# Transposing gated keys with a 112 × 112 identity in place of a 128 × 128 one, in an HGRN2 attention feeding a bilinear FFN

## The chip, the cores and the metric

The kernel runs on one NeuronCore of one Trainium2 chip. The metric is the device time of one execution in microseconds (us). Before the change it is 597.28 us, the median of three runs (597.1 to 597.85).

## What is computed

The first part is a linear attention with a gate per channel, for 4 batches × 8 heads, 768 tokens, head width 48. Its output, put back into rows of 384 channels, goes through a bilinear feed-forward block (384 → 1536 → 384). All of it is float32, with the FFN weights arriving as doubles.

```python
f = 1.0 / (1.0 + np.exp(-f_logit))
for t in range(S):
    state = f[:, :, t, :, None] * state + np.einsum('bhd,bhe->bhde', k[:, :, t], v[:, :, t])
    y[:, :, t] = np.einsum('bhd,bhde->bhe', q[:, :, t], state)
x = y.transpose(0, 2, 1, 3).reshape(B * S, H * D)
out = (x @ w_a) * (x @ w_b) @ w_out
```

## The kernel before

**Units and their places.** `by_quotients` cuts the attention into 16 units u = 0 to 15: four heads times one block of 384 tokens each. In SBUF a unit's q, k and f are tiles of 128 partitions × 2 × 384. Two heads lie above each other, the one in partitions 0 to 47 and the other in 64 to 111 (R = 64, D = 48); the rows 48 to 63 and 112 to 127 hold padding. v lies with its tokens on the partitions. The names carry the set of buffers that a unit uses, u modulo 3: `k_in` of unit 9 is that of set 0, of unit 10 set 1, of unit 11 set 2.

**The front of a unit** (`front_parts`, lines 302 to 347) makes sigmoids on ScalarE (L312, L315), an affine step on GpSimd (L318), running products and sums as scans on VectorE (L322, L335), and multiplies k and q by them on VectorE (L339). After that the attention of a chunk of 128 tokens is plain matrix products.

**The core of a unit.** `scores` (L392) multiplies k with q in 24 small matrix products and `mask` (L405, VectorE) copies the causal part into `at`. `turn` (L416) transposes the unit's decayed keys, so that tokens come to lie on partitions: 6 TensorE transposes a unit, each with a 128 × 128 block of k as the stationary operand and the identity as the moving one, into one pair of PSUM banks. `turned` (L423 for units 0 and 1, L425 for the others) copies the pair on ScalarE into the SBUF tile `kT`, [128 tokens, 2, 3 chunks, 128]. `gains` (L440) multiplies a 48-column slice of `kT` with v; it reads the columns 0 to 47 and 64 to 111 of a chunk and no others. `carried` or `carry` (L467, L469) sums the gains into running states on VectorE. `within` (L489) and `across` (L515) make the outputs, and `out_of_bank` (L534) with DMAs brings them into `xT`.

**The FFN.** Blocks 0 and 1 of 384 tokens use plain products (`up`, L598, and `product`, L618 and L620). From block 2 on, `up_triples` (L714 to 791) does the product of a 3 × 3 by a 3 × 2 block matrix with 15 multiplications in place of 18. For each of four columns j it makes 15 named products v1, v6 (of the column before), u1, r2, v2, u2, t1, v3, u3, r3, v4, u4, t2, v5, u5, in that order. One named product is one "beat": two matmuls of 192 columns. They go into four PSUM banks (in turn called v, u, r, t), are copied out by ScalarE (`copy`, shown as L1307, where the planner emits it) or added by VectorE (`add` and others, L712), and the next product that uses the bank has to wait for that. `down` (L795, matmuls at L822) multiplies by w_out, two blocks of 128 tokens at a time.

**What sets the order.** Up to unit 3 the order is written out by hand (lines 1002 to 1120). From there a small planner (lines 1138 to 1310) walks along a main list of FFN steps and fills in the attention's steps from lines of their own. It keeps a clock of its own for TensorE (`now`) and for each other engine, adds each step's stated cost to it, and emits a step of a side line when it fits. In `core_parts` (line 901) each step has its cost in nanoseconds: `scores` 1000, `turn` 850, `turned` 700, `gains` 1000. These numbers are no instructions; they decide only where steps stand in the queues. Each engine then runs its own queue in that order, and waits at semaphores.

Of the kernel before, what the change touches and what calls it, by code (L numbers as in the profile page):

```python
# [12 lines left out]
FP32 = mybir.dt.float32  # L13
# [7 lines left out]
C = 128  # L21
FINE = (0, 1, 2, 4, 8, 16)
BLK = 384
# [3 lines left out]
R = 64  # L27
# [115 lines left out]
def by_quotients(ctx, tc, q, k, f_logit, v, moe_w_a, moe_w_b, moe_w_out, out, ident, weights, bad, ps_f):  # L143
    nc = tc.nc
    B, H, D, S = q.shape
# [5 lines left out]
    NC = BLK // C  # L151
# [9 lines left out]
    sb1 = ctx.enter_context(tc.tile_pool(name="sb1", bufs=1))  # L161
# [39 lines left out]
    def unit(u):  # L201
        b, r = divmod(u, NH * NQ)
        return (b, *divmod(r, NQ))
# [89 lines left out]
    PE, DVE, ACT, POOL, SP = range(5)  # L293
    live = {}
# [4 lines left out]
    def halves(x):  # L299
        return x.rearrange("p n s -> p (n s)")  # L300
# [75 lines left out]
    def away(u):  # L376

        return ps_y if u == 2 else ps_x

    def pair_of(x):  # L380

        return [x[:, i] for i in range(2)]
# [25 lines left out]
    def turn(u):  # L408

        kf = halves(sets[u % NSET]["k"])  # L410
        live.setdefault(u, {})["kT"] = sb1.tile([128, 2, NC, 128], FP32, tag="kT", name="kT")
        ps = live[u]["turned"] = [ps_f[idle.pop(0)] for _ in range(2)] if u in FIRST else pair_of(away(u))
        for n in range(2):
            for c in range(NC):
                o = n * BLK + c * C
                nc.tensor.transpose(ps[n][:, c * C:c * C + C], kf[:, o:o + C], ident)  # L416

    def turned(u):

        kT, ps = live[u]["kT"], live[u]["turned"]  # L420
        if u in FIRST:
            for n in range(2):
                nc.scalar.copy(kT[:, n].rearrange("s c x -> s (c x)"), ps[n][:, 0:BLK])  # L423
        else:
            nc.scalar.copy(kT.rearrange("s n c x -> s n (c x)"), away(u)[:, :, 0:BLK])  # L425

    def gains(u, chunks=range(NC)):

# [112 lines left out]
    def stores_of(u):  # L541

        b, half, qd = unit(u)
        blk = b * NH + half

        def begin():
            if qd == 0:
                xT[blk] = sb2.tile([128, NKT, BLK], FP32, tag="xT", name="xT")
            live.pop(u - NQ, None)

        def store(n, h, kt, p, row, w):
            y = live[u]["y_sb"].rearrange("r (n c) p m -> r n (c p m)", n=2)
            queue = nc.sync if u != NQ - 1 else nc.gpsimd if n else nc.scalar
            queue.dma_start(out=xT[blk][p:p + w, kt], in_=y[row:row + w, n])

        yield begin
        for n in range(2):
            for h in range(2):
                ch, row, left = (4 * qd + 2 * n + h) * D, R * h, D
                while left:  # L560
                    kt, p = divmod(ch, 128)
                    w = min(left, 128 - p)
                    yield partial(store, n, h, kt, p, row, w)
                    ch, row, left = ch + w, row + w, left - w
# [336 lines left out]
    def core_parts(s):  # L901


        u = s - 1
        if u < 2 * NQ:
            yield PE, 1000, 0, scores, s
        elif s < NU:
            yield PE, 1600, 0, within_and_scores, u
        else:
            yield PE, 1000, 20 * BEAT, within, u  # L910
        if s < NU:
            yield DVE, 880, 0, mask, s
            yield PE, 850, 0, turn, s
            yield ACT, 700, 0, turned, s
        if u < 2 * NQ:
            yield PE, 1000, 0, gains, s
        elif s < NU:
            yield PE, 1550, 0, gains_and_across, u
        else:
            yield PE, 1000, 0, across, u  # L920
        if s < NU:
            for j in range(NJ - 1 if unit(s)[1] == NH - 1 else NJ):
                yield DVE, 180, 0, carry, s, j
            if unit(s)[1] < NH - 1:
                yield DVE, 320, 0, hand_on, s
        if u >= 2 * NQ:
            for part in range(3):
                yield ACT, 490, 0, out_of_bank, u, part
            begin, *stores = stores_of(u)
            yield SP, 0, 0, begin  # L930
            for do in stores:
                yield SP, ISSUE, 5000, do
# [41 lines left out]
    with tc.manual_schedule():  # L974
# [43 lines left out]
        begin(1)  # L1018
        keep_up(2)
        turn(0)  # L1020
        turned(0)
        scores(0)
        begin(2)
        gains(0)
        keep_up(4)
        for _ in range(3):
            next(fronts[1])
        turn(1)
        turned(1)
        mask(0)  # L1030
        scores(1)
# [154 lines left out]
        for s in range(2 * NQ, NU + 1):  # L1186
            if s < NU:
                loaded = ()
                if s - NSET in stores:
                    at = stores[s - NSET]  # L1190
                    loaded = (loads.extend([(SP, ISSUE, 6000, do) for do in loads_of(s)], needs=(at,)),)
                ready = fore.extend(
                    [(e, load, 0, *do) for part in front_parts(s) for e, load, *do in part], needs=loaded
                )
            for step in core_parts(s):
                blk, second = divmod(s - 1, NQ)
                core.extend(
                    (step,),
                    needs=(ready,) if step[3] in (scores, within_and_scores) else (),
                    past=behind[blk - 2] if step[3] in (across, gains_and_across) and not second else 0,  # L1200
                )
            if s > 2 * NQ:
                stores[s - 1] = core, len(core.steps)
            if s > 2 * NQ and s % NQ == 0:
                blk = s // NQ - 1
                one_by_one = combine_x(blk)
                marks["x", blk] = for_x.extend(
                    [(e, load, 0, next, one_by_one) for e, load in X_STEPS],
                    needs=(stores[s - 1],),
                    past=behind[blk - 1] if blk > 2 else behind["down"],  # L1210
                )
# [448 lines left out]
```

## Time and profile before

| | |
|---|---|
| median of three runs | 597.28 us |
| the profiled execution, as a run | 596.37 us |
| span of the profiled execution | 594.6 us |
| TensorE matmuls busy | 572.6 us (96%) |
| VectorE busy | 412.2 us (69%) |
| ScalarE busy | 268.7 us (45%) |
| mean granted TensorE clock | 0.997 |

The profile is of one execution. The run's time is 1.8 us longer than its span, which begins with the first instruction and ends with the last. A matmul in full float32 has two records in the profile (L598 has 288 for 144 calls); a transpose has one (L416 has 96 for 16 units × 6). The pieces of the chain of waits count a weight load and a matmul each, so that "x4" of L598 there is two passes; in the timeline of one engine "x4" of L720 is one beat. In units of work "PE" is the matmul and "PEld" the weight load that runs beside it.

### The profile page before, as it was taken

To read this page: it belongs to the slowest core of one execution; us is meant where nothing else is said; L and a number is where in the kernel's file an instruction comes from. 1 tells how busy PE (TensorE), PEld (TensorE's weight loads), DVE (VectorE), ACT (ScalarE), POOL (GpSimd) and SP (SyncE) were. 2 spreads that over 40 slices of the span, in tenths; PEclk is the share of its full clock that TensorE was granted. 3 is DMA by queue.
4 is the path that set the end of the run, shared out by engine and by line. 5 is a ranking of instruction groups with operands and counts; after the bars stand their busy time and mean duration, and the time that the engine had idled before them with its cause. 6 is when DMAs were issued, how large, how long until landed. Compare 5 with 4: busy or idle time off the path is not lost.

```text
span 594.6 us, 13952 instructions
## 1 busy us (share of the span) xinstructions
PE 572.6 (96%) x5802; PEld 512.9 (86%) x5802; DVE 412.2 (69%) x786; ACT 268.7 (45%) x507; POOL 77.7 (13%) x71
## 2 busy tenths in 40 slices
PE   2899999999999999999999999999999999999997
PEld 1655655557999999999999999999999999999996
DVE  6899545599978678958894678847785165836751
ACT  6589959753132464245521444326431345135300
POOL 6254425355000000000000000000000000000000
PEclk9899999999999999999999999999999999999999
DMA  9696699089542440044004410041001100000001
GB/s 211 183 267 197 213 273 268 0 147 186 116 141 71 115 93 10 15 120 95 2 1 125 108 23 2 2 105 43 3 1 47 48 1 0 2 28 1 0 29 33
DMA packets 33561, 49.43 MB, mean 83 GB/s; under 512 B 3984, under 2 KB 25264, under 8 KB 33488
## 3 DMA queue, kind: packets, MB, share of 16 engines
q1 hardware_dynamic: 30000, 42.19, 25.5%
q0 software_dynamic: 3056, 5.92, 5.9%
q8 instruction: 47, 0.77, 0.5%
q10 hardware_dynamic: 432, 0.34, 0.2%
q14 instruction: 26, 0.21, 0.1%
HBM read 33.23 MB, written 4.72 MB: 64 GB/s over the span
## 4 chain that ended last, share of the span: by engine, by line
PE 85%; DVE 10%; issue 2%; ACT 1%; DMA 1%; SPq 0%; DVEq 0%; ACTq 0%
PE ps_f L720 35%; PE ps_f L822 28%; PE ps_f L598 13%; PE ps_y L489 2%; DVE inv L335 2%; PE ps_y L515 2%; PE ps_x L392 2%; PE ps_x L440 1%; PE ps_x L416 1%; DVE sums L712 1%; DVE groups L712 1%; DVE spare L335 1%; DVE q_in L339 1%; DVE f_in L322 1%; DVE w_ba L73 1%
## 5 line engine op out<-in xcount | busy, mean ns | idle before, releaser
L598 PE MATMUL ps_f<-xT,w_ba 128*128 128x384 f32 x288 | 95.6, 489 | 1.5 <-DMA xT<-y 1.4
L1307 ACT COPY sums<-ps_f 128x384 f32<-128x384 f32 x120 | 57.4, 480 | 75.9 <-PE ps_f L720 68.2
L598 PEld LDWEIGHTS ps_f<-xT,w_ba 128*128 128x128 f32 x288 | 53.8, 190 | 38.2 <-issue 2.2
L1307 ACT COPY groups<-ps_f 128x384 f32<-128x384 f32 x120 | 57.7, 481 | 62.9 <-PE ps_f L720 39.9
L720 PE MATMUL ps_f<-xT,w_ba 128*128 128x192 f32 x384 | 78.4, 327 | 0.0
L720 PEld LDWEIGHTS ps_f<-xT,w_ba 128*128 128x128 f32 x384 | 64.7, 190 | 0.2
L720 PE MATMUL ps_f<-groups,w_ba 128*128 128x192 f32 x288 | 55.5, 327 | 0.0
L720 PE MATMUL ps_f<-x_sums,raw 128*128 128x192 f32 x288 | 54.1, 331 | 1.2 <-DVE groups L712 0.9
L822 PE MATMUL ps_f<-w_out,sums 128*128 128x192 f32 x288 | 52.2, 329 | 0.3 <-DVE groups L620 0.3
L822 PE MATMUL ps_f<-w_out,groups 128*128 128x192 f32 x288 | 51.7, 328 | 0.0
L720 PEld LDWEIGHTS ps_f<-x_sums,raw 128*128 128x128 f32 x288 | 46.9, 190 | 4.3 <-DVE groups L712 1.8
L822 PE MATMUL ps_f<-spare,sums 128*128 128x192 f32 x288 | 49.0, 326 | 0.0
L720 PEld LDWEIGHTS ps_f<-groups,w_ba 128*128 128x128 f32 x288 | 47.8, 190 | 0.5 <-ACT groups L1307 0.3
L822 PEld LDWEIGHTS ps_f<-w_out,sums 128*128 128x128 f32 x288 | 47.1, 190 | 1.3 <-DVE groups L620 0.6
L318 POOL TENSOR_SCALAR inv<-inv 128x768 f32<-128x768 f32 x14 | 13.1, 935 | 266.7 <-ACT inv L315 266.7
L822 PEld LDWEIGHTS ps_f<-w_out,groups 128*128 128x128 f32 x288 | 47.1, 190 | 0.7
L822 PEld LDWEIGHTS ps_f<-spare,sums 128*128 128x128 f32 x288 | 47.1, 190 | 0.1
L60 POOL TENSOR_SCALAR sums<-sums 128x768 f32<-128x768 f32 (+1 forms) x20 | 40.4, 2018 | 43.9 <-ACT sums L58 43.8
L712 DVE TENSOR_TENSOR sums<-sums,groups 128x768 f32<-128x768 f32 x36 | 34.7, 965 | 14.2 <-ACT groups L1307 13.7
L712 DVE TENSOR_TENSOR sums<-ps_f,sums 128x384 f32<-128x384 f32 x60 | 32.8, 553 | 16.5 <-PE ps_f L720 15.0
L720 PE MATMUL ps_f<-x_sums,w_ba 128*128 128x192 f32 x192 | 39.3, 327 | 0.5 <-DVE sums L712 0.5
L720 PE MATMUL ps_f<-xT,raw 128*128 128x192 f32 x192 | 39.4, 328 | 0.0
(142 smaller groups left out, 869.3 us busy)
## 6 DMA issues: line engine op xcount, KB each, us to landing
raw<-w_ba POOLq DMA_DIRECT2D x11, 512.0 KB, 8.6
k_in<-in_k_dram SPq DMA_DIRECT2D x32, 144.0 KB, 4.2
q_in<-in_q_dram SPq DMA_DIRECT2D x32, 144.0 KB, 4.4
v_in<-in_v_dram SPq DMA_DIRECT2D x16, 288.0 KB, 5.0
raw<-in_moe_w_out_dram SPq DMA_DIRECT2D x6, 768.0 KB, 5.9
out_dram<-o SPq DMA_DIRECT2D x22, 192.0 KB, 1.9
f_in<-in_f_logit_dram SPq DMA_DIRECT2D x28, 144.0 KB, 3.0
xT<-y SPq DMA_DIRECT2D x45, 72.0 KB, 2.2
```

The source lines that it names most:

```text
L60: nc.gpsimd.tensor_scalar(h, h, HI_MAX, None, ALU.min)
L73: nc.vector.tensor_tensor(dst[:, rows], hu[:, rows], bit[:, rows], ALU.add)
L318: nc.gpsimd.tensor_scalar(inv, inv, EXP_K, 1.0, ALU.mult, ALU.add)
L335: nc.vector.tensor_tensor_scan(inv[:, w], inv[:, w], none[:, 0:C], first, ALU.mult, ALU.add)
L392: nc.tensor.matmul(ps[h][SUB * p:SUB * p + SUB, o:o + SUB], lhsT=kf[r, tokens(n, c, p)], rhs=qf[r, tokens(n, c, p)], start=True, stop=True,)
L489: nc.tensor.matmul(ps[p][e:e + D, o:o + SUB], lhsT=t["v"][r, n, c, h * D:h * D + D], rhs=at[r, h, o:o + SUB], start=o == 0, stop=True, ski ...
L515: nc.tensor.matmul(ps[p][e:e + D, o:o + SUB], lhsT=st[j][r, n], rhs=qf[r, tokens(n, c, p)], start=False, stop=True, skip_group_check=True,)
L598: nc.tensor.matmul(ps[nm][:, 0:BLK], lhsT=w[:, kt, ft * 128:ft * 128 + 128], rhs=xT[blk][:, kt], start=kt == 0, stop=kt == NKT - 1,)
L712: nc.vector.tensor_tensor(to, x, y, op)
L720: nc.tensor.matmul(ps[:, g], lhsT=sums_of_w[name][:, g, 128 * j:128 * j + 128], rhs=sums_of_x[blk][name], start=start and g == 0, stop=Tru ...
L822: nc.tensor.matmul(to, lhsT=x[:, i // 2, i % 2], rhs=w[:, NI * (i % 2) + i // 2], start=start and i == 0, stop=i == HFT - 1, skip_group_ch ...
L1307: do(*args)
```

## The change

The transposes read 112 rows of k and 112 × 112 of the identity; the chunks of the turned keys follow each other at 112 columns in PSUM and in `kT`, and the copies move 2 × 336 elements a partition in place of 2 × 384. The stated cost of `turn` in the planner goes from 850 to 760.

```diff
-        live.setdefault(u, {})["kT"] = sb1.tile([128, 2, NC, 128], FP32, tag="kT", name="kT")
+        live.setdefault(u, {})["kT"] = sb1.tile([128, 2, NC, R + D], FP32, tag="kT", name="kT")
         ps = live[u]["turned"] = [ps_f[idle.pop(0)] for _ in range(2)] if u in FIRST else pair_of(away(u))
+        used = ident[0:R + D, 0:R + D]
         for n in range(2):
             for c in range(NC):
                 o = n * BLK + c * C
-                nc.tensor.transpose(ps[n][:, c * C:c * C + C], kf[:, o:o + C], ident)
+                nc.tensor.transpose(ps[n][:, c * (R + D):(c + 1) * (R + D)], kf[0:R + D, o:o + C], used)
...
-                nc.scalar.copy(kT[:, n].rearrange("s c x -> s (c x)"), ps[n][:, 0:BLK])
+                nc.scalar.copy(kT[:, n].rearrange("s c x -> s (c x)"), ps[n][:, 0:NC * (R + D)])
         else:
-            nc.scalar.copy(kT.rearrange("s n c x -> s n (c x)"), away(u)[:, :, 0:BLK])
+            nc.scalar.copy(kT.rearrange("s n c x -> s n (c x)"), away(u)[:, :, 0:NC * (R + D)])
...
-            yield PE, 850, 0, turn, s
+            yield PE, 760, 0, turn, s
```

A comparison of the built queues of both kernels shows what moves. With the new sizes and the old 850, no instruction changes place. With 760, the queues differ in two places of TensorE, both in the planner's part: around unit 9's outputs and unit 10's turn (256 to 263 us in the profile before), where a beat of `up_triples` (v1) comes ahead of `within`, `scores` and what follows; and around unit 10's outputs and unit 11's turn (285 to 291 us), where `within`, `scores` and `turn` come one beat earlier. VectorE's and ScalarE's queues change around the same places by a few steps each.

## The prediction

> **What bounds the kernel.** I read the page first, its busy shares and the chain that ended last.
>
> ```profile
> PE 572.6 (96%) x5802; PEld 512.9 (86%) x5802; DVE 412.2 (69%) x786; ACT 268.7 (45%) x507; POOL 77.7 (13%) x71
> PE 85%; DVE 10%; issue 2%; ACT 1%; DMA 1%; SPq 0%; DVEq 0%; ACTq 0%
> ```
>
> TensorE is the bound: 96% busy, 85% of the chain. The rest of the chain is mostly VectorE: the start up to 50.8 us, where TensorE waits anyway, and three short stretches (222 to 228, 287 to 302, 346 to 357 us). So a transpose off TensorE's queue counts from 50.8 us on, unless VectorE gives the pace just then. Next the rows of the transposes and of their copies:
>
> ```profile
> L416 PEld LDWEIGHTS ps_x<-ident,k_in x78: 139/141/146, 54.5 to 427.3; 128*128 128x128 f32 x78
> L416 PE MATMUL ps_x<-ident,k_in x78: 272/273/273, 54.8 to 427.4; 128*128 128x128 f32 x78
> ```
>
> ```profile
> L425 ACT COPY kT<-ps_x x13: 771/798/818, 56.2 to 427.7; 128x768 f32<-128x768 f32 x13
> ```
>
> The 273 ns are one record's length, not what a transpose costs in a stream. That is read in the timeline of TensorE, from start to start:
>
> ```profile
> 289.67 0.82 PE L416 MATMUL ps_x<-ident,k_in 128*128 128x128 f32 x6
> 290.33 2.35 PE L720 MATMUL ps_f<-x_sums,raw 128*128 128x192 f32 x12
> ```
>
> Six transposes take 290.33 - 289.67 = 0.66 us; the chain gives 0.65 to 0.67 for others, so one step is 109 ns. The row below it is three beats of `up_triples`, usually 2.11 us (at 268.41 and 278.16) and here 2.35: 0.24 us of waiting lie in it. The chain of the same stretch:
>
> ```profile
> 286.95 0.75 PE ps_x L392 x47
> ...
> 288.60 0.95 DVE f_in L322
> 289.55 0.91 DVE sums L712 x2
> 290.46 0.87 DVE f_in L322
> ...
> 291.92 1.32 DVE sums L712 x2
> ...
> 293.32 0.48 ACT groups L1307
> 293.80 0.39 ACT sums L1307
> ...
> 300.53 1.03 DVE groups L712 x2
> 301.55 0.04 issue
> 301.60 1.41 PE ps_f L720 x7
> ```
>
> Here VectorE is full, and TensorE stands idle for 0.86 us ahead of 301.60. But the chain enters VectorE from TensorE, by the scores at 286.95: what TensorE saves before this stretch moves all of it.
>
> **What the Trainium skill says.** "TensorE: Matmul & The Clock Gate", section "LDWEIGHTS (loading the stationary operand)": a weight load takes columns / 1.2 ns, whatever the number of rows. The trace agrees for ordinary weights: 122, 134 and 190 ns for 48, 64 and 128 columns, some 0.85 ns a column above a fixed part. For the transposes it gives less, 141 ns for 128 columns. So cutting the rows of k from 128 to 112 saves nothing in the load; only the moving columns count. Its section "Back-to-back issue gap" has N / 2.4 + 2.5 ns for a lone bf16 stream and says that load and matmul set the spacing together. The trace's float32 passes are slower and the trace decides: 162.5 ns for 192 columns (a beat of 4 passes in 0.65 us), 109 for 128, thus (162.5 - 109) / 64 = 0.84 ns a column. Its "Part 4: PE-mode transpose" gives about 275 ns for a transpose in a kernel; the record here has 273.
>
> **The change, part by part.**
>
> *Transposes.* 16 moving columns fewer at 0.84 ns are 13.4 ns for one, if the stream sets the pace. For it: the steps of 128 and 192 columns lie on one line, the load of a transpose (141 ns long, 60 above the fixed part of the ordinary loads, 122 - 48 x 0.85 = 81) is shorter than its stream. Against: the load of the ordinary matmul behind the sixth has to hide behind a stream of 95 ns in place of 109, and 128 columns at 0.85 are 109. So a turn saves 5 x 13.4 = 67 ns up to 6 x 13.4 = 80; I take 75. The turns of units 0, 1 and 2 (at 13, 19 and 38 us) lie where VectorE makes the chain: nothing, and if that cover were gone, 0.08 us each. The 13 turns of units 3 to 15 save 13 x 0.075 = 0.98 us (0.87 to 1.04).
>
> *Copies.* 482 ns for 384 elements and 798 for 768: 0.82 ns an element, so 672 take 719, 79 ns less. ScalarE is 45% busy and other beats lie between turn and gains, so this hides nearly everywhere. It is on the chain once: at 346.2 the copy of unit 13 stands ahead of the sigmoid L315, the sigmoid ahead of the copies that VectorE needs up to 357.27. I count 0.08 us once (0 to 0.2). If the cover were gone in all 14, 1.1 us more would be saved.
>
> *Reading columns.* `gains` reads the same values at a step of 112 columns; same shapes, nothing.
>
> *The planner's 760.* GpSimd's queue stays as it is, SyncE's keeps its order too; no DMA passes another. Around 256 us a beat (v1) comes ahead of unit 9's `within` and unit 10's `scores`. TensorE has no stall from 256 to 286, and its work there is the same; the mask behind waited 1.34 us, and takes the shift. The copy of the keys then comes some 0.5 us ahead of its gains, as before. Nothing.
>
> Around 286 us `within`, `scores` and `turn` of unit 11 come a beat earlier. Placed by hand with the durations of the trace (before the other savings): `within` 285.35, scores end 287.04 in place of 287.69; the mask waits for them and starts at 287.08, not 287.73. Behind it on VectorE stands now the addition of r3, which before filled the wait (0.46 us). One scan that stood ahead of the k product has moved into an idle 0.34 us at 280.5, so k and q are ready some 0.35 us earlier, by 284.9. Then the scans and additions follow as before: the addition of u4 ends at 289.74, where u5 wants its bank at 290.15. On ScalarE the copy of the keys is done by 290.4, so that the copy of v5 (before from 291.22, with v6 waiting for it: the 0.24 us above) is done by 290.8, and v6 is due at 291.45: that wait goes. VectorE's second addition at 292.29 comes at 291.9 to 292.0. From there to the wait ahead of 301.60 the order is the same, so v1 of the next column starts some 0.3 to 0.4 us earlier. I take 0.38 us. Late next is VectorE itself: the stall before v1 is still about 0.7 us. Bounds: all of it, 0.86 + 0.24 = 1.1 us gained, or 0.6 lost if the moved steps meet a bank a beat too late.
>
> *Sum.* 0.98 + 0.08 + 0.38 = 1.44 us. The span goes from 594.6 to 593.1, the run that was profiled from 596.37 to 594.9. The median of the runs shown is 0.91 us above that run; I take the difference off the median: 597.28 - 1.44 = 595.84, and say 595.8.
>
> 0.2% is 1.19 us, about what a measurement of this kernel can tell from no change.
>
> **Rivals.**
>
> *The load sets the pace.* The stationary operand keeps 128 columns, and 128 at 0.85 ns are 109 ns, just the step that is seen. Then 112 moving columns save nothing, and there remain 0.08 + 0.38: 596.8 us. For it: the agreement of the numbers. Against it: the transposes' own load record, 49 ns shorter than an ordinary one. 0.11.
>
> *VectorE takes it back.* What is saved ahead of a VectorE-bound stretch is waited away in it: turns 3 to 13 count for nothing, the two behind 357 us save 0.15, with 0.08 and 0.38: 596.7 us. For it: three stretches where TensorE waits for VectorE. Against: each of them is entered from TensorE, at 222.2 by a copy, at 287.7 by the scores, at 346.2 by the copy of the keys. 0.14.
>
> *The new order makes a wait (slower).* Place: VectorE's queue at 287 us, the mask ahead of the additions of r3, u4 and t2. If the scores wait for unit 11's products, the mask holds these back, and u5 waits for its bank. It decides from q being late past 286.1, against 284.9 expected; each us past that is a us on TensorE up to 301 us. With k, an addition and q still ahead (0.88 + 0.87 + 0.87 = 2.62 us) the sum is 2.62 - 1.44 = 1.18 lost: 598.5 us. Against it: 1.2 us of slack. 0.07.
>
> *The change is not what it says.* A block of 112 rows might not run as a transpose in one pass: an ordinary float32 matmul has two records, a transpose one. Two passes of 95 ns against 109 cost 81 ns x 6 x 13 = 6.3 us: 603.6 us. Nothing in the trace speaks for it. 0.02.
>
> **How the numbers follow.** The forecast has 0.66, with a range of its own from 594.9 to 596.7 (the order's bounds, narrowed, since both ends need everything to go one way); 0.47 of it is below 596.09 and so faster by over 0.2%, 0.19 within. The first two rivals are within 0.2% (0.11 + 0.14), the third half so (0.03), and 0.04 of it with the last 0.02 slower. Faster 0.47, same 0.47, slower 0.06. The range takes in the two rivals and the scatter of the runs (0.75 us): 594.9 to 597.4; above lie the last two rivals (0.09), below some 0.05.
>
> **What would show it.** Right: L416 records of some 260 ns, six starting within 0.57 to 0.59 us; L425 at 719 ns; from 50 to 222 us a gap that grows by 0.07 to 0.08 us with each turn; the three beats behind unit 11's turn back at 2.11 us or so, and the wait ahead of the next v1 at 0.5 to 0.8 us. Wrong: six transposes still in 0.65 us (the first rival), a wait before u5 or within the beats around 290 us (the third), waits at 228, 301 and 357 us that have grown by what was saved before them (the second), 192 records of L416 (the last).

## The result and the profile after

The changed kernel takes 595.62 us (median of 22 runs) and the kernel before, run beside it, 597.06. The ratio is 0.9976, with a 95% interval from 0.9966 to 0.9986: 1.4 us faster (0.8 to 2.0). One of the 22 runs of the kernel before took 747.74 us and is left out of the ratio. The forecast was 1.44 us. The profiled execution has a span of 593.8 us against 594.6; single spans scatter by more than that (18 runs of the kernel before, beside one of the experiments, go from 593.2 to 596.0 us), so the traces are compared stage by stage.

In the changed kernel all lines behind 410 have numbers one higher. First the rows of the transposes and of their copies (length as min/median/max in ns), then the timeline of TensorE:

```profile
L417 PEld LDWEIGHTS ps_x<-ident,k_in x78: 137/140/145, 54.2 to 426.1; 112*128 112x128 f32 x78
L417 PE MATMUL ps_x<-ident,k_in x78: 257/259/262, 54.5 to 426.2; 112*128 112x112 f32 x78
```

```profile
L426 ACT COPY kT<-ps_x x13: 693/719/737, 55.9 to 426.5; 128x672 f32<-128x672 f32 x13
```

```profile
276.79 0.81 PE L721 MATMUL ps_f<-xT,w_ba 128*128 128x192 f32 x4
277.59 2.22 PE L721 MATMUL ps_f<-x_sums,raw 128*128 128x192 f32 x12
...
288.54 0.74 PE L417 MATMUL ps_x<-ident,k_in 112*128 112x112 f32 x6
289.12 0.83 PE L721 MATMUL ps_f<-xT,w_ba 128*128 128x192 f32 x4
289.78 2.11 PE L721 MATMUL ps_f<-x_sums,raw 128*128 128x192 f32 x12
...
300.79 1.57 PE L721 MATMUL ps_f<-x_sums,raw 128*128 128x192 f32 x8 [0.86 <-DVE groups L713]
```

The weight load of a transpose has stayed, 140 ns. Its matmul is 14 ns shorter, and six of them take 289.12 - 288.54 = 0.58 us in place of 0.66. The beat behind them takes 0.83 us where other beats take 0.81: some of the gain is given back at once (how much is worked out below). The three beats behind unit 11's turn are at 2.11 us, not 2.35. But there is a new wait: the beat at 276.79 is done after 0.65 us, at 277.44, and u5 starts at 277.59 and runs into a group of 2.22 us. And the wait ahead of 300.79 is 0.86 us, as it was ahead of 301.60.

### The profile page after: what moved, and what is told of

It reads as the page before. It is cut to its first block, busy times and chain, and to the rows that moved or that the text cites. A ratio compares the mean times of both kernels' runs of the same rounds, so it can differ in the third digit from the quotient of the medians.

```text
span 593.8 us, 13951 instructions
## 1 busy us (share of the span) xinstructions
PE 573.3 (97%) x5802; PEld 513.1 (86%) x5802; DVE 411.9 (69%) x786; ACT 267.8 (45%) x507; POOL 77.1 (13%) x71
## 4 chain that ended last, share of the span: by engine, by line
PE 85%; DVE 11%; issue 2%; ACT 1%; DMA 1%; SPq 0%; DVEq 0%; ACTq 0%
PE ps_f L721 35%; PE ps_f L823 28%; PE ps_f L599 13%; PE ps_y L490 2%; PE ps_y L516 2%; DVE inv L335 2%; PE ps_x L392 2%; DVE sums L713 1%; PE ps_x L441 1%; PE ps_x L417 1%; DVE groups L713 1%; DVE spare L335 1%; DVE q_in L339 1%; DVE f_in L322 1%; DVE w_ba L73 1%
```

## The experiments

Times of experiments with a ratio are medians beside runs of the kernel before on the same chip; the others are one run with its profile. A stage is the time from the start of one piece of the chain of waits to the start of a later one, the same two pieces in each profile. The columns are the kernel before; this kernel with the smaller copies alone, with the smaller transposes alone, with both sizes in the old order, and with the new order alone; the changed kernel; and its second profile. The stages lasted, in us:

| stage (us in the profile before) | before | copies | transposes | sizes | order | both | both again |
|---|---|---|---|---|---|---|---|
| 50.8 to 149.0, turns 3 to 5 | 98.12 | 98.08 | 97.93 | 97.87 | 98.08 | 97.87 | 97.85 |
| 149.0 to 150.3, no turn | 1.39 | 1.66 | 1.46 | 1.72 | 1.67 | 1.73 | 1.71 |
| 150.3 to 228.5, turns 6 to 8 | 78.11 | 78.11 | 77.94 | 77.92 | 78.11 | 77.92 | 77.91 |
| 228.5 to 242.0, turn 9 | 13.56 | 13.57 | 13.49 | 13.49 | 13.56 | 13.52 | 13.50 |
| 242.0 to 304.5, turns 10, 11 | 62.49 | 62.45 | 62.46 | 62.47 | 62.14 | 62.13 | 62.17 |
| 304.5 to 336.0, turn 12 | 31.46 | 31.46 | 31.40 | 31.40 | 31.46 | 31.40 | 31.40 |
| 336.0 to 357.3, turn 13 | 21.30 | 21.22 | 21.22 | 21.14 | 21.30 | 21.14 | 21.14 |
| 357.3 to 440.9, turns 14, 15 | 83.64 | 83.67 | 83.50 | 83.54 | 83.68 | 83.51 | 83.55 |
| 440.9 to 576.3, no turn | 135.38 | 135.37 | 135.38 | 135.37 | 135.38 | 135.37 | 135.38 |
| behind 576.3, to the end | 18.31 | 18.32 | 18.90 | 17.19 | 18.54 | 18.68 | 18.58 |

The two profiles of the changed kernel agree within 0.04 us in each row down to 576 us, and rows whose work is the same in two kernels differ by up to 0.04 us too, so that smaller differences are not read. The tail and the start (50.2 to 51.4 us over all profiles) scatter by more than that; so what the turns of units 0 to 2 are worth cannot be seen. The pause at 149 us is left out of the sums as well. That matters: with it in, the sizes come to 0.53 us and not 0.86, as the kernel before has the shortest pause of all. The other two kernels with its transposes (copies, order) have 1.66 and 1.67, near those with the new sizes. The times from the first plain products to the last down products, further below, contain the pause.

### The sizes alone

```diff
-            yield PE, 760, 0, turn, s
+            yield PE, 850, 0, turn, s
```

(against the changed kernel; here and in the other runs made from it, the name `used` is also written out in the call)

> The new sizes (112 rows and columns, copies of 672) with the old planner cost of 850, so that no instruction changes place. If the stream of the moving columns sets the pace of a transpose and the order was worth some 0.2 to 0.4 us: 1.0 to 1.1 us faster than before, ratio about 0.9982; six transposes in 0.58 us on the chain; the three beats behind unit 11's turn still at 2.35 us, the wait behind them too. If the new order brought the gain and the sizes next to nothing: ratio 0.9995 to 1.0005. If VectorE takes the savings back in its stretches: some 0.3 us, ratio 0.9995, with waits at 228, 301 and 357 us grown by 0.4 us and more.

595.5 us against 596.73, ratio 0.9982 (0.9974 to 0.9989): 1.1 us (0.7 to 1.6). Over the stages, leaving the pause and the tail out, it is 0.86 us. As expected of the first theory; both others fall as an account of the whole. The wait in the beats behind unit 11's turn has stayed, and grown: from the start of the three beats to the second beat behind them it is 2.93 us (289.70 to 292.63), before 2.85 (290.33 to 293.18). That is the 0.08 us that the turn had saved.

### The order alone

```diff
-            yield PE, 850, 0, turn, s
+            yield PE, 760, 0, turn, s
```

(against the kernel before)

> The old sizes with the planner's 760: the new order alone. If the order is worth what the two traces show (0.2 us won around 255 us, 0.24 lost at 277.5 where u5 waits for the addition of u4, 0.24 won behind unit 11's turn): 0.1 to 0.4 us faster, ratio 0.9993 to 0.9998, not told from no change; six transposes in 0.65 us; the three beats behind unit 11's turn at 2.11 us, and a u5 at 277 to 278 us that waits for VectorE. If the order brought the whole gain: ratio 0.9976.

596.75 us against 596.73, ratio 0.9997 (0.9988 to 1.0007): not told from no change. The trace shows what it is: 0.35 us, all of it between 242 and 304 us, and both the loss at 277 to 278 us and the gain at 291:

```profile
278.43 2.22 PE L720 MATMUL ps_f<-x_sums,raw 128*128 128x192 f32 x12
...
290.69 2.11 PE L720 MATMUL ps_f<-x_sums,raw 128*128 128x192 f32 x12
...
301.62 1.57 PE L720 MATMUL ps_f<-x_sums,raw 128*128 128x192 f32 x8 [0.86 <-DVE groups L712]
```

```profile
278.43 1.76 PEld L720 LDWEIGHTS ps_f<-x_sums,raw 128*128 128x128 f32 x11 [0.28 <-DVE groups L712]
```

The second fence is the weight load's own view (PEld): there the wait of u5 for VectorE's addition L712 is named, 0.28 us, which the matmul's record hides. In the profile before, the first and the last of these groups of beats were:

```profile
278.16 2.12 PE L720 MATMUL ps_f<-x_sums,raw 128*128 128x192 f32 x12
...
301.60 1.57 PE L720 MATMUL ps_f<-x_sums,raw 128*128 128x192 f32 x8 [0.86 <-DVE groups L712]
```

0.86 (sizes) and 0.35 (order) make 1.21; both together show 1.20 and, in a second profile, 1.16. So the parts add up, and the 0.2 us between them and the measured 1.4 are within its interval.

### What sets the pace of a transpose

```diff
+        rows = {4: 128, 5: 112, 6: 96, 7: 80, 8: 64, 9: 48, 10: 32, 12: 112, 14: 64, 15: 128}.get(u)
+        for i in range(12 if rows else 0):
+            o = i % NC * C
+            nc.tensor.transpose(ps[i % 2][:, o:o + rows], kf[0:rows, o:o + C], ident[0:rows, 0:rows])
```

(in `turn` of the kernel before, ahead of its six)

> The kernel before, with twelve more transposes ahead of the six of ten units, whose results the six then overwrite: of 128 rows in units 4 and 15, of 112 in 5 and 12, 96 in 6, 80 in 7, 64 in 8 and 14, 48 in 9, 32 in 10; all have 128 stationary columns. If the stream of moving columns sets the pace: start to start 109 ns for 128, 95 for 112, 82 for 96, 68 for 80, down to the pace of the load, which I put at 60 ns or less, so that 64, 48 and 32 lie near 55 to 60. If the load of 128 columns sets the pace at 0.85 ns a column: 109 ns for all. If only the loads of ordinary matmuls are that slow: the first beat behind the six starts no later than before.

In this kernel the added transposes are L416 and the kernel's own six are L420:

```profile
133.02 1.47 PE L416 MATMUL ps_x<-ident,k_in 128*128 128x128 f32 x12
134.33 0.82 PE L420 MATMUL ps_x<-ident,k_in 128*128 128x128 f32 x6
...
147.90 1.32 PE L416 MATMUL ps_x<-ident,k_in 112*128 112x112 f32 x12
149.06 0.82 PE L420 MATMUL ps_x<-ident,k_in 128*128 128x128 f32 x6
...
163.41 1.16 PE L416 MATMUL ps_x<-ident,k_in 96*128 96x96 f32 x12
164.41 0.82 PE L420 MATMUL ps_x<-ident,k_in 128*128 128x128 f32 x6
...
193.71 1.00 PE L416 MATMUL ps_x<-ident,k_in 80*128 80x80 f32 x12
194.54 0.82 PE L420 MATMUL ps_x<-ident,k_in 128*128 128x128 f32 x6
...
210.20 0.96 PE L416 MATMUL ps_x<-ident,k_in 64*128 64x64 f32 x12
211.09 0.88 PE L420 MATMUL ps_x<-ident,k_in 128*128 128x128 f32 x6
...
264.90 0.93 PE L416 MATMUL ps_x<-ident,k_in 32*128 32x32 f32 x12
265.76 0.87 PE L420 MATMUL ps_x<-ident,k_in 128*128 128x128 f32 x6
```

606.31 us in its one run. From the start of each row to the start of the next, divided by twelve, it is 109 ns for 128 columns, 97 for 112, 83 for 96, 69 for 80, then 74 for 64 and 72 for 48 and 32. The last three hold pauses at the two ends of the run. Narrow windows inside the runs give the step itself:

```profile
193.78 0.72 PE L416 MATMUL ps_x<-ident,k_in 80*128 80x80 f32 x8
210.38 0.60 PE L416 MATMUL ps_x<-ident,k_in 64*128 64x64 f32 x7
264.99 0.72 PE L416 MATMUL ps_x<-ident,k_in 32*128 32x32 f32 x9
```

With the length of the last record off (233, 227 and 224 ns) and divided by the 7, 6 and 8 steps that remain, that is some 70, 62 and 62 ns; single records give 95 to 97 ns for 112 columns and 68 to 70 for 80. So down to 80 columns the stream sets the pace, at 0.84 ns a column, as forecast. Below lies a floor of 62 ns, just above the 60 that I gave as its upper end. The 128 stationary columns are what stays the same there, while their rows fall with the moving columns; that the load of these columns makes the floor fits, but no run tests it apart. The runs of 64 columns and fewer also begin and end with a pause: the run starts 256 ns after the pass ahead of it in place of 163, and the last step takes 151 to 154. From the start of the twelve to the beat behind the six it is 1.60 us with 64 columns and 1.49 with 80. The rival by which the load holds every transpose at 109 ns falls.

### The copies alone

```diff
-            nc.scalar.copy(kT.rearrange("s n c x -> s n (c x)"), away(u)[:, :, 0:BLK])
+            nc.scalar.copy(kT[:, :, :, 0:R + D], away(u)[:, :, 0:BLK].rearrange("s n (c x) -> s n c x", c=NC)[:, :, :, 0:R + D])
```

(in the kernel before)

> The kernel before, with the copies of units 2 to 15 alone cut to the 112 columns that are read (three runs of 112 out of every 128). The copy takes 719 ns, or a little more for the added dimension, in place of 798. If it counts only where it stands ahead of unit 13's sigmoid: the stretch from unit 13's transposes to the beats behind 357 us is 0.08 us shorter than before and every other interval between the pieces of the chain is as before; one run cannot show 0.08 us in its total. If ScalarE's copies were on the path at each turn: 1 us in all, 0.08 at each.

596.34 us in its one run. The copies take 719 ns, the runs of 112 cost nothing more, and the stage of unit 13's turn is 21.22 us, 0.08 shorter. All other stages but the pause are within 0.04 of the kernel before.

### The transposes alone

```diff
-                nc.tensor.transpose(ps[n][:, c * C:c * C + C], kf[:, o:o + C], ident)
+                w = C if u in FIRST else R + D
+                nc.tensor.transpose(ps[n][:, c * C:c * C + w], kf[0:w, o:o + C], ident[0:w, 0:w])
```

(in the kernel before)

> The old order and full copies of 768 elements, with transposes of 112 rows and columns for units 2 to 15 alone (units 0 and 1 stay at 128). Columns 112 to 127 of each chunk of the copy are then leftovers that nobody reads. Each turn of units 3 to 10, 12, 14 and 15 saves 0.07 to 0.08 us to the next piece of the chain. Unit 13's stretch (from the beats ahead of its transposes to the beats behind 357 us, 13.90 us before, 13.74 with sizes) is 13.82: the transposes' half of it. Unit 11's turn lies within VectorE's stretch and saves nothing: from the scores to the next v1, 14.65 us before, it stays 14.65. If all 13 turns counted as I forecast, 14.57.

596.45 us in its one run. Unit 13's stage is 21.22, 0.08 shorter, and with the 0.08 of the copies the sizes' 21.14 is made exactly. The stage with turns 10 and 11 is 62.46: 0.03 us, no more than the scatter, and not the 0.15 of two turns. The other eleven turns together win 0.19 + 0.17 + 0.07 + 0.06 + 0.08 + 0.14 = 0.71 us, 0.065 each.

### Is unit 11's turn on the path?

```diff
-        for n in range(2):
+        for n in [*range(2), *range(2 if u in (11, 12) else 0)]:
```

(in `turn` of the kernel with the new sizes and the cost 850: the six are done twice)

> The new sizes in the old order, with the six transposes of units 11 and 12 done twice (the same results): six more steps of 96 ns, 0.58 us, in each of the two turns. If unit 11's turn lies inside a stretch to which VectorE gives the pace, its 0.58 us vanish in the wait of 0.86 us ahead of the next v1: from the down products at 242 us to those at 304 us 62.47 us as with the sizes alone, the wait ahead of v1 some 0.3 us; and unit 12's show in full: from 304 to 336 us 31.40 + 0.58 = 31.98. If unit 11's turn is on the path as I forecast, both grow by 0.58.

597.25 us in its one run. From 242 to 304 us it takes 62.47 us, as without the six added; from 304 to 336 us 31.98, 0.58 more. Unit 11's added 0.58 us cost nothing, unit 12's cost all of it. These are the ends of the two stages in the chain, first with the sizes alone, then here:

```profile
241.49 14.20 PE ps_f L822 x84
303.96 12.55 PE ps_f L822 x76
335.36 5.85 PE ps_f L720 x36
```

```profile
242.36 14.20 PE ps_f L822 x84
304.83 12.55 PE ps_f L822 x76
336.81 5.85 PE ps_f L720 x36
```

And the timeline of TensorE around unit 11's turn:

```profile
290.00 1.32 PE L416 MATMUL ps_x<-ident,k_in 112*128 112x112 f32 x12
291.15 2.27 PE L720 MATMUL ps_f<-x_sums,raw 128*128 128x192 f32 x12
...
301.92 1.57 PE L720 MATMUL ps_f<-x_sums,raw 128*128 128x192 f32 x8 [0.70 <-DVE groups L712]
```

The wait ahead of v1 fell from 0.86 to 0.70 us only, not to 0.3: the other 0.42 went into smaller waits of the beats between. The stage of unit 13 came to 21.28 us against 21.14: its scores took 0.14 us longer, for no reason that the profile shows.

### The changed kernel again

The name `used` is written out in the call, so that line numbers stay those of the kernel before; nothing else differs.

> The changed kernel once more, for the scatter of single profiles: the start of the first plain products at 50.5 us, the pause between gains and across near 149 us (0.48 us in the profile before, 0.81 after), and the tail behind the last matmul. If these are scatter, they differ by 0.2 to 0.4 us from the first profile of the same kernel; if they belong to the change, they come again within 0.05 us.

595.89 us in its one run. The start is at 51.01 us against 50.53 in the first profile of the same kernel: scatter. The pause at 149 us is 1.71 against 1.73; but the kernel before with only its copies cut has 1.66, with only its order changed 1.67, with only its transposes cut 1.46. So 1.39 and 1.46 are not the mark of the old sizes; what makes the pause is not shown by any wait in the profile, and stays open. It differs by 0.35 us at most.

### Other costs for the planner

First a lower cost of the turn:

```diff
-            yield PE, 760, 0, turn, s
+            yield PE, 700, 0, turn, s
```

> The new sizes with a stated cost of 700: on TensorE only the first of the two places changes (v1 ahead of unit 9's outputs), the second stays as before; VectorE's queue differs in a few steps. From the start of the down products at 242 us to those at 304 us the kernel before takes 62.49 us, the changed one 62.13, the sizes alone 62.47, the order alone 62.14. If the first place brings the 0.2 us at 255 and the second brings the end of the wait behind unit 11's turn: 62.25 to 62.35 here, with the wait of 0.24 us in the three beats behind unit 11's turn still there, or lost in VectorE's stretch. If the second place alone counts at 301 us: 62.45 or more.

596.21 us in its one run. The stage is 62.01 us, 0.48 shorter than before, better than I had from either place alone, but the stage from 150 to 228 us is 78.57, 0.65 longer than with the sizes. The second is a new wait elsewhere, in a stretch that I had not looked at: TensorE waits for VectorE's additions for 0.9 us there, in two places, where with the sizes it waits for 0.5 in one. The run says that a place is not worth a fixed amount.

Then the cost that the turn was measured at:

```diff
-            yield PE, 760, 0, turn, s
+            yield PE, 580, 0, turn, s
```

> The new sizes with the cost that a turn is now measured at, 580 ns. The planner then moves steps in some six places of TensorE's queue instead of two. If the order counts only by luck of single waits: within 0.5 us of the changed kernel either way, ratio to before 0.997 to 0.9985. If a true cost makes better plans: 0.5 us and more under the changed kernel, ratio below 0.997.

594.96 us against 596.67, ratio 0.9971 (0.9962 to 0.998). From the first plain products at 50.8 us to the last down products it takes 524.02 us, where the kernel before takes 525.45 and the changed one 524.59: 0.6 us better than the changed kernel in the trace. The ratio lies on the border of the two expectations and its interval takes in both.

Then all costs of the core's steps:

```diff
-            yield PE, 1000, 0, scores, s
+            yield PE, 820, 0, scores, s
...
-            yield PE, 1600, 0, within_and_scores, u
+            yield PE, 1560, 0, within_and_scores, u
...
-            yield PE, 760, 0, turn, s
-            yield ACT, 700, 0, turned, s
+            yield PE, 580, 0, turn, s
+            yield ACT, 720, 0, turned, s
...
-            yield PE, 1000, 0, gains, s
+            yield PE, 690, 0, gains, s
...
-            yield PE, 1550, 0, gains_and_across, u
+            yield PE, 1360, 0, gains_and_across, u
```

(`within` and `across` of the last unit: 1000 to 820)

> The new sizes, with the planner's costs of all of the core's steps at about what the trace shows: scores 820, within 820, both 1560, turn 580, its copy 720, gains 690, across 820, gains with across 1360. If true costs make better plans: faster than with 580 for the turn alone, ratio to before under 0.9965. If the order counts by single waits that a cost doesn't know of: anywhere between 0.9965 and 0.9995, with new waits of TensorE for VectorE in one or two places.

593.89 us against 596.61, ratio 0.9958 (0.9944 to 0.9972): 2.5 us (1.7 to 3.3), and by the trace the shortest version tried. From 50.2 us to the last down products: 522.48 us. In the profile's windows from 128 to 440 us TensorE is idle for 1.22 us, before for 2.53. The plan is better here, by 1.5 us of the trace than with 580 for the turn alone (522.48 against 524.02). That true costs make better plans in general is not shown by one plan; the run with 700 shows that a new order can also lose 0.65 us.

Last, the same costs in the kernel before, with its transposes of 128 and its copies of 768:

> The order of the kernel with true costs (the same numbers, turn 580 too, so that every instruction stands where it stood there), with the old transposes of 128 and copies of 768. If the sizes are worth 0.8 us and the order the rest of the 2.5 us, each for itself: 1.6 to 1.8 us faster than before, ratio about 0.9971. If the order needs the shorter turns: less, ratio 0.998 or above.

594.84 us against 597.5, ratio 0.9953 (0.9933 to 0.9973). The interval is wide and takes in the expected 0.9971; the time alone cannot tell the two versions apart. The traces can: 523.30 us from the first plain products to the last down products, against 522.48 with the new sizes. So the costs alone are worth 525.45 - 523.30 = 2.15 us, and the sizes 0.82 us on top, about as much as in the old order (0.86). The order did not need the shorter turns.

## Why the prediction was right

The time was met, but its terms less well: one was too large and one came about by other steps than I gave. The terms measured in the traces make 0.74 + 0.08 + 0.35 = 1.17 us where I had 1.44. The interval of the measured time, 0.8 to 2.0 us, takes in both sums; that its middle lies within 0.04 us of mine is luck.

**Transposes: mechanism right, size too large.** The stream sets the pace: inside a turn the transposes start 95 to 96 ns apart, where I had 95, against 109 before. Two things in the term of 0.98 us were off. First, a turn was put at 75 ns, between 67 and 80; it is 65. In the single records six transposes take 577 ns in place of 655, 78 less. But the second pass of the beat behind them then starts 178 ns after the first, in place of 165, and 13 ns are lost again. The weight load of that pass starts 110 ns after the load before it, in both kernels, while the loads of the transposes have come down from 109 to 96 ns apart. This is what I had put under "Against", with 109 ns for an ordinary load; no run changed that load alone, so it fits and is not proved. Second, 13 turns were counted, where 12 are worth something at most: unit 11's lies behind the scores by which the chain enters VectorE's stretch, not ahead of them. I had read that the chain enters by the scores at 286.95 and that the turn is at 289.67, and drew the line at the wrong side of the turn. The added transposes settle it. In the old order a further 0.05 us seems to be taken back at 253 us, where the last down group waits for VectorE: the down products from 242 us on last 14.20 us in all three profiles of this order with the new transposes, 14.12 and 14.15 in the two without. Transposes alone: 0.74 us.

**Copies: right**, 719 ns and 0.08 us, in the one place named. There the limit has moved: with the new transposes the profile puts the wait of unit 13's copy down to an addition of VectorE, which ends at about the same time as they do (345.84 and 345.83 us with the transposes alone; the copy starts at 345.86). Whether still shorter transposes would win anything at this place is not shown.

**Order: sum right by luck, way partly wrong.** 0.35 us against 0.38. The wait behind unit 11's turn went as placed by hand. In the changed kernel the gain from there to the next v1 is 0.33 us: the beat at 283.37 of the profile before stands at 282.89, 0.48 earlier, and v1 at 300.79 in place of 301.60, 0.81 earlier. But the wait ahead of v1 did not shrink to 0.7; TensorE came earlier by as much as VectorE did. The step that failed is "One scan that stood ahead of the k product has moved into an idle 0.34 us at 280.5". It moved further, ahead of the additions of u4 and t2 at 277 us, and u5, which wants u4's bank, waits: 0.24 us lost. I also had "Nothing" for the first place. There an addition of the down products (L857, in the changed kernel L858) came ahead of a scan, and the last group of `down` no longer waits for it. Its weight loads before and after:

```profile
253.95 1.92 PEld L822 LDWEIGHTS ps_f<-w_out,sums 128*128 128x128 f32 x12 [0.25 <-DVE o L857]
```

```profile
253.24 1.98 PEld L823 LDWEIGHTS ps_f<-w_out,sums 128*128 128x128 f32 x12
```

From the start of the group ahead to `within` it was 4.29 us (251.81 to 256.10). With the order alone it is 4.70 (252.18 to 256.88), of which 0.65 are the beat v1 that now stands between: 0.24 us won. That is as much as the other missed step lost; they cancel, and the sum was left as I had it.

**Rivals.** That the load sets the pace: refuted by the doses. That VectorE takes it back: right for unit 11's turn and perhaps for 0.05 us at 253, wrong for the others; the stretches at 222 and 346 us let the savings through, as their chains are entered behind the turns. The new order did make a wait, but at another place and a tenth of the price given.

## What to carry to other kernels

A saving on the bounding engine counts only if it lies ahead of the point at which the chain goes over to another engine: find the instruction by which the chain enters the other engine's stretch, and count nothing that stands behind it until the chain comes back. A cost that a planner keeps is an edit of its own: build the old order with the new sizes and the new order with the old sizes, and compare stages between the same pieces of the chain, which here showed 0.08 us where whole runs could not tell 0.35 from nothing. And measure all costs of a planner in the trace before tuning one of them: all of them together were worth 2.15 us in the one plan tried here, more than the change.

## What the runs showed of the hardware

Inside a run, single-pass float32 transposes with 128 stationary columns started 109 ns apart with 128 moving columns, 95 with 112, 69 with 80, and 62 with 64, 48 and 32. Runs of 64 columns and fewer had pauses at their ends, so that twelve of 64 columns, with the kernel's own six behind them, took 1.60 us in all and twelve of 80 took 1.49. A wait of TensorE cost more than its length: the group of three beats that begins after the wait at 278.43 takes 2.22 us, where the groups without a wait take 2.11.
